# First token transform in 64 points on two row tiles, gate on four column tiles, column 0 turned by TensorE

## The chip, the core and the metric

The kernel runs on one core of a Trainium2 chip. The core has TensorE (PE in the profile, with its weight loads as PEld), VectorE (DVE), ScalarE (ACT), GpSimd (POOL) and SyncE (SP, which here only issues DMAs). The metric is the device time of one execution in microseconds, and of several runs the median.

## The reference, cut to what matters

The input x has 2048 tokens by 1024 channels. Two branches read it, and a gate for each token mixes them.

```
X = rfft2(x) * (w_r + 1j*w_i);  a = irfft2(X)                    # spectral branch
Bu = x @ B_bar.T;  h[t] = Lam_bar * h[t-1] + Bu[t]               # state branch
b = 2 * real(h @ C.T) + x * Dskip
g = sigmoid(sum(x * gate_w, -1));  out = g * a + (1 - g) * b
```

## The kernel before, in words

**Layout.** A token s is written as s = 16 p + j: partition p (128), row j (16). Each row j of x is loaded with 128 tokens on the partitions (`load_x`, L197, two rows at a time, eight loads), transposed by TensorE and copied by ACT into `xQ` (`turn_x`, L651).

**Spectral branch, front.** For each row j, `fold` (L657, DVE) and `fd` (L334) do the transform over channels: matmuls into `ps_fd` and a copy by ACT to X1. Then `s1` (L348) does the first transform over tokens: 128 points over p, with the twiddles in the constant `T3` (cosine, sine, minus sine; loaded by `load_T3` into the tile `raw`). Four matmuls of 512 columns, lines 351 to 354, give a real and an imaginary half. The result is copied to A1 (L356; by DVE for j < 10, by ACT after), of which there are four buffers, and stored to a scratch in DRAM (L358, `turn_scratch` in the profile). From there it is read back with the tokens turned, and `s2` (L457) does the second transform, of 16 points, as a matmul with the constant K2; then comes the product with the weights, and the way back through a second scratch (steps "is1" and "is2").

**Column 0.** The first channel frequency packs two real columns and has its own path: `keep_A1` (L362) collects it in Acol; POOL sends Acol to DRAM and reads it back turned as Bcol (L369, L372); the matmuls `zps` (L417 to L420) with the constant `K3` do the second transform for it, and a chain of small DVE operations and matmuls (`Zp`, `Zrev`, `Q`, `Qn`) leads to the column that `s2` puts into X2.

**State branch.** `unit(c, q)` (L255) works on 256 tokens and half of the states: 64 matmuls in two halves into `psu` (L303, the moving operand is 16 runs of 16 tokens out of `xQ`), each copied by ACT to h (L305), then about 13 us of DVE work in seven pieces (rotation, two scans of 2.3 us, rotation back). The pieces are queued in `work` with a cost written by hand, and `vector(us)` (L314) emits pieces until as many microseconds are paid. `c_half` (L562) multiplies h with C into `ps_y`; `early` (L577) stores ten tiles' results for later, and the rest is joined with the spectral result at the end.

**Gate.** `gate(r0, n)` (L695) is called after rows 9, 11, 13 and 15, with four rows each: eight matmuls a row, with 128x128 of `xQ` as weights and one moving column, then a copy to `zsb` (L701). After the last one POOL sends `zsb` to DRAM (L703) and reads it back as `zt`, by token tiles (L705). `gate_end` (L707) turns `zt` into the factors gB, omg and grat; the copies `ye` of the early tiles (L586) need omg.

**Order.** On PE, DVE and ACT the order is the program's own: the work is under `manual_schedule`, and the text from L860 on interleaves a row of the front, one half of a unit or tile (`halves`) and the vector pieces by hand. The strings in `plan` (L771) say which of turn (T), fold (f), fd (F) and s1 (S) a row does; `order` (L763) says after which row the B, C and small constants are loaded. The order of the DMAs on SP and POOL is chosen when the kernel is built, from simulated times, and need not be that of the text: SP issues loads of B (L208, transposing DMAs) ahead of stores that the text has earlier. After the front, `step()` drives the spectral generator: "w" (halves of the weights' column and five half steps of the state branch), "z", "q", "qn", "s2", and so on.

**Memory.** The front's tiles lie in pools that are closed after row 15 (`after_ia`, L515), and the pools of the next stage take their place. PSUM: two slots `psA` for the spectral branch, one `psF` for the units in the front, two `psX` for transposes and the gate.

Of the kernel before, what the change touches and what calls it, by code (L numbers as in the profile page):

```python
# [13 lines left out]
FP32 = mybir.dt.float32  # L14
# [22 lines left out]
def _host_consts():  # L37

    d = np.arange(K)[:, None] + 0.5
    G = np.zeros((2, K, 2, H))  # L40
    for cls in range(2):
        k = 2 * np.arange(H)[None, :] + cls
        ang = 2 * np.pi * d * k / D
        G[cls, :, 0] = np.cos(ang)
        G[cls, :, 1] = -np.sin(ang)
    G[0, :, 1, 0] = (-1.0) ** np.arange(K)

    n = np.arange(H)[None, :] + 0.5
    Gi = np.zeros((2, 2, 2, P, H))
    for cls in range(2):  # L50
        for kb in range(2):
            k = 2 * (P * kb + np.arange(P)[:, None]) + cls
            ang = 2 * np.pi * k * n / D
            Gi[cls, kb, 0] = 2.0 * np.cos(ang)
            Gi[cls, kb, 1] = -2.0 * np.sin(ang)
    Gi[0, 0, 0, 0] = 1.0
    Gi[0, 0, 1, 0] = (-1.0) ** np.arange(H)
    Gi /= float(D * S)
    s1 = np.arange(P)[:, None, None]
    s2 = np.arange(16)[None, :, None]  # L60
    m1 = np.arange(P)[None, None, :]
    angT = 2 * np.pi * (((16 * s1 + s2) * m1) % S) / S
    Tc, Ts = np.cos(angT), np.sin(angT)
    p = np.arange(P)
    q = p // 8
    a = p % 8
    angK = 2 * np.pi * ((q[:, None] * q[None, :]) % 16) / 16
    delta = (a[:, None] == a[None, :]).astype(np.float64)
    Kc, Ks = delta * np.cos(angK), delta * np.sin(angK)
    f = np.arange(P)  # L70
    fs, fr, fa = f[:, None] // 8, (f[:, None] // 4) % 2, f[:, None] % 4
    hr, hm, ha = f[None, :] // 64, (f[None, :] // 4) % 16, f[None, :] % 4
    angF = 2 * np.pi * ((fs * hm) % 16) / 16
    K2 = (fa == ha) * np.where(fr == hr, np.cos(angF), np.where(fr == 1, 1.0, -1.0) * np.sin(angF))
    pp = (np.arange(P) % 64)[:, None, None]
    bb = np.arange(32)[None, :, None]
    nn = np.arange(64)[None, None, :]
    angM = 2 * np.pi * (((32 * pp + bb) * nn) % S) / S
    top = (np.arange(P) < 64)[:, None, None]
    Mre = np.where(top, np.cos(angM), -np.sin(angM))  # L80
    Mim = np.where(top, np.sin(angM), np.cos(angM))
    gr, gb, ga = f // 64, (f // 2) % 32, f % 2
    angR = 2 * np.pi * ((gb[:, None] * gb[None, :]) % 32) / 32
    R2 = (ga[:, None] == ga[None, :]) * np.where(gr[:, None] == gr[None, :], np.cos(angR),
                                                  np.where(gr[:, None] == 0, 1.0, -1.0) * np.sin(angR))
    R2 = R2.reshape(P, 64, 2).transpose(0, 2, 1).reshape(P, P)
    Sel = np.zeros((P, 2, 2, P))
    for h in range(2):
        for ri in range(2):
            Sel[2 * np.arange(64) + h, h, ri, 64 * ri + np.arange(64)] = 1.0  # L90
    J = np.zeros((P, P))
    J[np.arange(P), 127 - np.arange(P)] = 1.0
    P0 = np.zeros((P, P))
    P0[(128 - np.arange(P)) % 128, np.arange(P)] = 1.0
    b16 = lambda z: np.ascontiguousarray(np.asarray(z, dtype=np.float32).astype(ml_dtypes.bfloat16))
    return dict(
        Ge=b16(G[0, 0:H].reshape(2, P, 2, P, 2).transpose(1, 4, 0, 2, 3)),
        Go=b16(G[1].reshape(4, P, 2, P, 2).transpose(1, 0, 4, 2, 3)),
        Gi=b16(Gi.reshape(8, P, H).transpose(1, 0, 2)),
        T3=b16(np.stack([Tc, Ts, -Ts], axis=2)),  # L100
        K3=b16(np.stack([Kc, Ks, -Ks], axis=1)),
        MT=b16(np.concatenate([-Mim, Mre, Mim], axis=2)),
        KRS=b16(np.concatenate([K2, R2, Sel.reshape(P, 4 * P)], axis=1)),
        JP=b16(np.stack([J, P0], axis=1)),
    )
# [3 lines left out]
def kernel(  # L109
# [25 lines left out]
    cT3 = nc.inline_tensor(hc["T3"], name="c_T3").ap()  # L135
# [7 lines left out]
    turn1_dram = dram.tile([16, 2, P, K], BF16, name="turn1_scratch")  # L143
    turn2_dram = dram.tile([32, P, K], BF16, name="turn2_scratch")
    col0_dram = dram.tile([P, 16, 2], BF16, name="col0_scratch")
    z_dram = dram.tile([P, 16], FP32, name="z_scratch")
# [43 lines left out]
    x_v = x.rearrange("(p j) d -> p j d", j=16)  # L190
# [4 lines left out]
    fft["T3"] = raw.rearrange("p (j t m) -> p j t m", t=3, m=P)  # L195

    def load_x(i):  # L197
        nc.sync.dma_start(out=xn[i], in_=x_v[:, 2 * i:2 * i + 2, :])

    def load_T3(a, b):  # L200
        nc.sync.dma_start(out=fft["T3"][:, a:b], in_=cT3[:, a:b])

# [50 lines left out]
    work = []  # L253

    def unit(c, q):  # L255
# [43 lines left out]
        for ri in range(2):  # L299
            psu = pools["u"].tile([P, 4, TC], FP32, name="psu", tag="psu")  # L300
            for j in range(4):
                for d8 in range(8):
                    nc.tensor.matmul(psu[:, j, :], lhsT=BT[4 * q + j][:, ri, d8, :],  # L303
                                     rhs=xQ[:, d8, :, 16 * c:16 * (c + 1)], start=(d8 == 0), stop=(d8 == 7))
            nc.scalar.copy(out=u[:, ri].rearrange("p b (q j) -> p b q j", j=16),  # L305
                           in_=psu.rearrange("p b (j q) -> p b q j", j=16))
# [23 lines left out]
    def gfnet():  # L330
        T3_sb = fft["T3"]
        Acol = fx.tile([P, 16, 2], BF16, name="Acol")
# [15 lines left out]
        def s1(j):  # L348
            X1 = X1s.pop(j)
            psa = psA.tile([P, 2, K], FP32, name="ps_s1", tag="ps")  # L350
            nc.tensor.matmul(psa[:, 0, :], lhsT=T3_sb[:, j, 0, :], rhs=X1[:, 0, :], start=True, stop=False)
            nc.tensor.matmul(psa[:, 0, :], lhsT=T3_sb[:, j, 1, :], rhs=X1[:, 1, :], start=False, stop=True)
            nc.tensor.matmul(psa[:, 1, :], lhsT=T3_sb[:, j, 0, :], rhs=X1[:, 1, :], start=True, stop=False)
            nc.tensor.matmul(psa[:, 1, :], lhsT=T3_sb[:, j, 2, :], rhs=X1[:, 0, :], start=False, stop=True)
# [3 lines left out]
            nc.sync.dma_start(out=turn1_dram[j].rearrange("r m k -> m r k"), in_=A1)  # L358
# [3 lines left out]
        def keep_A1(j):  # L362
            nc.vector.tensor_copy(out=Acol[:, j, :], in_=A1s[j][:, :, 0])
# [5 lines left out]
        nc.gpsimd.dma_start(out=col0_dram, in_=Acol)  # L369
        Bcol = fx.tile([P, 16, 2], BF16, name="Bcol")  # L370
        with nc.allow_non_contiguous_dma(reason="tiny corner turn"):
            nc.gpsimd.dma_start(out=Bcol, in_=col0_dram.rearrange("(a b) j c -> j a b c", a=8))  # L372
# [4 lines left out]
        Kc_sb, Ks_sb, Kns_sb = fft["K3"][:, 0], fft["K3"][:, 1], fft["K3"][:, 2]  # L377
        Wc = fft["Wc"]
        KRS_sb = fft["KRS"]
        t1_v = turn1_dram.rearrange("j r (a b) k -> (j r a) b k", a=4)  # L380
# [34 lines left out]
        yield "w"  # L415
        zps = psA.tile([P, 2, 16], FP32, name="zps", tag="ps")
        nc.tensor.matmul(zps[:, 0, :], lhsT=Kc_sb, rhs=Bcol[:, :, 0], start=True, stop=False)  # L417
        nc.tensor.matmul(zps[:, 0, :], lhsT=Ks_sb, rhs=Bcol[:, :, 1], start=False, stop=True)
        nc.tensor.matmul(zps[:, 1, :], lhsT=Kc_sb, rhs=Bcol[:, :, 1], start=True, stop=False)
        nc.tensor.matmul(zps[:, 1, :], lhsT=Kns_sb, rhs=Bcol[:, :, 0], start=False, stop=True)  # L420
# [94 lines left out]
    def after_ia():  # L515
# [7 lines left out]
        fft["wp"] = bctx.enter_context(tc.tile_pool(name="wp", bufs=1, side="right", reuse_waits="tile"))  # L523
        fft["Sel"] = fft["gt"].tile([P, 4, P], BF16, name="Sel_sb", tag="gc1", bufs=2)
# [152 lines left out]
    load_T3(0, 2)  # L677
    load_x(1)
    load_x(2)
    load_T3(2, 8)  # L680
    for i in range(3, 8):
        load_x(i)
    load_T3(8, 16)
# [8 lines left out]
    zsb = cpool.tile([P, 16], FP32, name="zsb")  # L692
    zt = cpool.tile([P, 16], FP32, name="zt")

    def gate(r0, n):  # L695
        zps = psX.tile([P, n], FP32, name="zps_g", tag="pt")
        for r in range(r0, r0 + n):
            for d8 in range(8):
                nc.tensor.matmul(zps[:, r - r0:r - r0 + 1], lhsT=xQ[:, d8, r, :], rhs=gwT[:, d8:d8 + 1],
                                 start=(d8 == 0), stop=(d8 == 7))  # L700
        nc.scalar.copy(out=zsb[:, r0:r0 + n], in_=zps)  # L701
        if r0 + n == 16:
            nc.gpsimd.dma_start(out=z_dram, in_=zsb)  # L703
            with nc.allow_non_contiguous_dma(reason="gate by token tiles"):
                nc.gpsimd.dma_start(out=zt, in_=z_dram.rearrange("(t a) j -> (a j) t", a=8))  # L705
# [14 lines left out]
    fft["K3"] = fx.tile([P, 3, P], BF16, name="K3_sb")  # L720
# [3 lines left out]
    def load_small():  # L724
        nc.sync.dma_start(out=fft["K3"], in_=cK3)
        nc.sync.dma_start(out=fft["JP"], in_=cJP)
        nc.sync.dma_start(out=fft["KRS"], in_=cKRS.rearrange("p (i m) -> p i m", m=P)[:, 0:2])
# [75 lines left out]
    gwT = vecT[:, 4]  # L803
# [56 lines left out]
    while at[0] < 16:  # L860
# [6 lines left out]
        if j in (9, 11, 13, 15):  # L867
            gate(2 * (j - 9), 4)
# [10 lines left out]
    for v, n in (("w", 5), ("z", 2), ("q", 2), ("qn", 1), ("s2", 0), ("uv", 1)):  # L879
# [91 lines left out]
```

## Time and profile before

| what | value |
|---|---|
| median of 7 runs | 348.69 us (347.09 to 350.62) |
| the profiled execution | 347.07 us, its span 345.3 us |
| PE busy | 329.0 us, 95% of the span |
| DVE busy | 298.0 us, 86% |
| ACT busy | 167.4 us, 48% |
| POOL busy | 34.4 us, 10% |
| mean granted clock of TensorE | 0.993 |
| DMA | 59.30 MB, 172 GB/s over the span |
| s1's matmuls, L351 to L354 | 64 of 128x512, 379 ns each as recorded, 0.215 us from start to start |
| gate's matmuls, L699 | 128 of one column, 163 ns each as recorded |
| psu's matmuls, L303 | 1024 of 256 columns, 117.7 us in all |

A matmul's record contains the way through the array, so records overlap; the cost of one in a stream is the distance of the starts. The chain of waits is read from the end backwards: each piece is what released the next. A DMA is on the queue of the engine that issued it; "DMA share" is the mean busy share of the core's 16 DMA engines, and may be over 1 where records overlap. "Released by" names what came last of the things that an instruction waited for.

### The profile page before, as it was taken

How to read it: one execution, taken by the hardware profiler on the slowest of the kernel's cores; microseconds unless marked ns; L12 is line 12 of the kernel's file. 1: busy time of each engine (PE TensorE's matmuls, PEld its weight loads, DVE VectorE, ACT ScalarE, POOL GpSimd, SP SyncE). 2: the span in 40 equal slices, each digit the busy share in tenths (PEclk: the TensorE clock that was granted, in tenths of full speed). 3: DMA queues.
4: the chain of work that ended last, by engine and by line, in shares of the span. 5: the costliest groups of instructions: out<-in, count | busy, mean ns of one | idle time of the engine just before them, and what ended most of it. 6: DMA issues, size and time to landing. Idle time of an engine off the chain costs nothing.

```text
span 345.3 us, 6604 instructions
## 1 busy us (share of the span) xinstructions
PE 329.0 (95%) x2593; PEld 226.8 (66%) x2593; DVE 298.0 (86%) x509; ACT 167.4 (48%) x215; POOL 34.4 (10%) x66
## 2 busy tenths in 40 slices
PE   7889599969999999999999999999999999999995
PEld 4666378858876675666647475596857885665652
DVE  2779687999997999999999999999646999999951
ACT  3798576575331225556646562365633333434410
POOL 1372011020021000000000000000000002112220
PEclk9999989999999999999999999999999999999999
DMA  7999999998793134869999953986601009866694
GB/s 289 392 219 177 222 211 201 188 243 213 232 195 49 63 91 100 248 186 248 294 205 308 238 163 107 245 186 166 178 2 61 2 0 163 133 103 130 116 153 151
DMA packets 83743, 59.30 MB, mean 172 GB/s; under 512 B 54368, under 2 KB 74496, under 8 KB 83584
## 3 DMA queue, kind: packets, MB, share of 16 engines
q1 hardware_dynamic: 80400, 56.20, 64.8%
q0 software_dynamic: 3232, 2.67, 8.1%
q8 instruction: 20, 0.33, 0.4%
q14 instruction: 11, 0.09, 0.1%
q10 hardware_dynamic: 80, 0.01, 0.0%
HBM read 31.06 MB, written 17.84 MB: 142 GB/s over the span
## 4 chain that ended last, share of the span: by engine, by line
PE 70%; DVE 16%; ACT 5%; DMA 5%; issue 3%; POOL 0%; ACTq 0%; DVEq 0%
PE ps_y L568 24%; PE psu L303 23%; PE ps_h L568 4%; PE ps_id L599 4%; DVE h L277 3%; PE ps_is L509 2%; PE ps_s L460 2%; PE ps_is L485 2%; PE ps_is L484 2%; ACT xQ L655 2%; DMA z_scratch<-zsb 2%; PE ps_y L572 2%; DVE A L356 1%; PE ps_fd L342 1%; DMA zt<-z_scratch 1%
## 5 line engine op out<-in xcount | busy, mean ns | idle before, releaser
L303 PE MATMUL psu<-xQ,BT 128*128 128x256 bf16 x1024 | 117.7, 275 | 3.9 <-ACT zsb L701 2.6
L303 PEld LDWEIGHTS <-BT 128*128 128x128 bf16 x1024 | 100.6, 99 | 20.4 <-issue 5.1
L568 PE MATMUL ps_y<-CT,h 128*128 128x512 bf16 x448 | 101.3, 379 | 0.0
L568 PEld LDWEIGHTS <-h 128*128 128x128 bf16 x512 | 49.6, 98 | 55.4
L277 DVE TENSOR_TENSOR_SCAN h<-rz,h 128x1024 bf16<-128x1024 f32 x32 | 72.4, 2281 | 0.3
L305 ACT CAST h<-psu 128x1024 bf16<-128x1024 f32 x32 | 32.3, 1010 | 57.8 <-PE psu L303 57.8
L614 POOL DMA_DIRECT2D BT<-y_scratch x10 | 12.1, 1206 | 211.9 <-ACT BT L602 178.1
L586 ACT ACTIVATE ye<-ps_y,omg 128x512 f32<-128x512 f32 x20 | 12.7, 684 | 33.1 <-PE ps_y L572 22.6
L264 DVE TENSOR_TENSOR su<-h,tab 128x2048 bf16<-128x2048 bf16 x16 | 19.6, 1223 | 8.0 <-ACT h L305 5.4
L462 ACT CAST X<-ps_s 128x1024 bf16<-128x1024 f32 x16 | 16.2, 1014 | 8.7 <-PE ps_s L460 8.7
L265 DVE TENSOR_TENSOR h<-h,tab 128x2048 bf16<-128x2048 bf16 x16 | 19.6, 1225 | 0.8
L290 DVE TENSOR_TENSOR h<-h,tab 128x2048 bf16<-128x2048 bf16 x16 | 19.6, 1225 | 0.5
L289 DVE TENSOR_TENSOR sg<-h,tab 128x2048 bf16<-128x2048 bf16 x16 | 19.5, 1218 | 0.0
L345 ACT CAST X<-ps_fd 128x1024 bf16<-128x1024 f32 x16 | 16.2, 1016 | 4.9 <-PE ps_fd L342 4.8
L511 ACT CAST ZT<-ps_is 128x1024 bf16<-128x1024 f32 x16 | 15.4, 1021 | 5.1 <-issue 3.0
L655 ACT COPY xQ<-pt 128x1024 bf16<-128x1024 bf16 x16 | 15.9, 1023 | 2.7 <-PE pt L654 2.7
L342 PE MATMUL ps_fd<-Go_sb,preT 128*128 128x256 bf16 x128 | 16.6, 273 | 0.0
L356 DVE CAST A<-ps_s 128x1024 bf16<-128x1024 f32 x10 | 12.2, 1218 | 4.8 <-DMA turn_scratch<-A 2.5
L487 ACT CAST C<-ps_is 128x1024 bf16<-128x1024 f32 x16 | 16.1, 1007 | 0.0
L599 PE MATMUL ps_id<-raw,ZT 128*128 128x256 bf16 x128 | 15.9, 273 | 0.0
L568 PE MATMUL ps_h<-CT,h 128*128 128x512 bf16 x64 | 14.5, 379 | 0.0
L599 PEld LDWEIGHTS <-ZT 128*128 128x128 bf16 x128 | 12.4, 98 | 2.2
(196 smaller groups left out, 414.4 us busy)
## 6 DMA issues: line engine op xcount, KB each, us to landing
y_scratch<-ye SPq DMA_DIRECT2D x20, 256.0 KB, 2.6
CT<-in_A_x_dram SPq DMA_DIRECT2D x8, 512.0 KB, 6.1
turn_scratch<-A SPq DMA_DIRECT2D x16, 256.0 KB, 4.4
Bb<-turn_scratch SPq DMA_DIRECT2D x16, 256.0 KB, 4.0
turn_scratch<-C SPq DMA_DIRECT2D x16, 256.0 KB, 2.7
raw<-turn_scratch SPq DMA_DIRECT2D x16, 256.0 KB, 4.4
Wb<-in_A_w_r_dram SPq DMA_DIRECT2D x32, 127.8 KB, 4.2
Wb<-in_A_w_i_dram SPq DMA_DIRECT2D x32, 127.8 KB, 3.8
```

Of the source, the lines that this page charges most:

```text
L264: nc.vector.tensor_mul(out=su, in0=u[:, ::-1], in1=bc(1))
L265: nc.vector.tensor_mul(out=u, in0=u, in1=bc(0))
L277: nc.vector.tensor_tensor_scan(out=seg, data0=rz[:, js].rearrange("p j t -> p (j t)"), data1=seg, initial=0.0, op0=ALU.mult, op1=ALU.add)
L289: nc.vector.tensor_mul(out=sg, in0=u[:, ::-1], in1=bc(3))
L290: nc.vector.tensor_mul(out=u, in0=u, in1=bc(2))
L303: nc.tensor.matmul(psu[:, j, :], lhsT=BT[4 * q + j][:, ri, d8, :], rhs=xQ[:, d8, :, 16 * c:16 * (c + 1)], start=(d8 == 0), stop=(d8 == 7))
L305: nc.scalar.copy(out=u[:, ri].rearrange("p b (q j) -> p b q j", j=16), in_=psu.rearrange("p b (j q) -> p b q j", j=16))
L342: nc.tensor.matmul(ps[:, q, H:K], lhsT=preTs[j][:, 4 + d4, :], rhs=fft["Go"][:, d4, q, :], start=(d4 == 0), stop=(d4 == 3))
L345: nc.scalar.copy(out=X1.rearrange("p r (i m) -> p r i m", m=4), in_=ps.rearrange("p q (c r i) -> p r i (q c)", c=2, r=2))
L568: nc.tensor.matmul(psy, lhsT=hs[c, jb // 4][:, ri, jb % 4, P * tq:P * (tq + 1)], rhs=CT[ri][:, jb, 512 * dh:512 * (dh + 1)], start=(i == 0 ...
L599: nc.tensor.matmul(pse[:, slot, :], lhsT=ZT_t[:, i, tb, :], rhs=fft["Gi"][:, i, :], start=(kb == 0), stop=(kb == 1))
L655: nc.scalar.copy(out=xQ[:, :, j, :], in_=pt)
```

## The change

A token is now s = 32 q + 16 g + j, and the partition of x is p = 64 g + q: the lower half of the partitions holds g = 0, the upper g = 1. The first transform has 64 points over q. Each half of the partitions is one row tile of the PE array (64 rows, 128 columns: real and imaginary part side by side), with a bank of PSUM of its own; two matmuls for each half take the place of the four over 128 rows. The constant T2 has two parts where T3 had three. The second transform has 32 points; K2 has other numbers and the same shape. x is loaded with two DMAs in place of each one. The unit's moving operand is 32 runs of 8 tokens.

The gate is one call after row 10 in place of four: gate_w is spread over 32 columns (gw32, a DVE copy), and four column tiles of 32 columns each take 512 tokens of `xQ` as moving operand, for eight blocks of channels: 32 matmuls. One copy by ACT and two DMAs of POOL follow at once.

Column 0: Acol is transposed by TensorE (`aps`), two DVE copies make Bcol (real, imaginary, minus real), and `zps` takes sixteen matmuls of 32 rows in place of four. The transpose and the copies are a step "a" of their own, one half step of the state branch ahead of "z"; "w" has four half steps in place of five. The constant K3 (64 KB) is loaded in `after_ia`, ahead of Sel, no longer after row 10.

```diff
-    turn1_dram = dram.tile([16, 2, P, K], BF16, name="turn1_scratch")
+    turn1_dram = dram.tile([32, P, K], BF16, name="turn1_scratch")
...
-    x_v = x.rearrange("(p j) d -> p j d", j=16)
+    x_v = x.rearrange("(p g j) d -> g p j d", g=2, j=16)
...
-    fft["T3"] = raw.rearrange("p (j t m) -> p j t m", t=3, m=P)
+    fft["T2"] = raw[:, 0:4 * D].rearrange("p (j t m) -> p j t m", t=2, m=P)
     def load_x(i):
-        nc.sync.dma_start(out=xn[i], in_=x_v[:, 2 * i:2 * i + 2, :])
+        for g in range(2):
+            nc.sync.dma_start(out=xn[i][64 * g:64 * (g + 1)], in_=x_v[g, :, 2 * i:2 * i + 2, :])
...
+    x_t = xQ.rearrange("p d j (g q) -> p d g j q", g=2)
...
-                                     rhs=xQ[:, d8, :, 16 * c:16 * (c + 1)], start=(d8 == 0), stop=(d8 == 7))
-            nc.scalar.copy(out=u[:, ri].rearrange("p b (q j) -> p b q j", j=16),
-                           in_=psu.rearrange("p b (j q) -> p b q j", j=16))
+                                     rhs=x_t[:, d8, :, :, 8 * c:8 * (c + 1)], start=(d8 == 0), stop=(d8 == 7))
+            nc.scalar.copy(out=u[:, ri].rearrange("p b (q j) -> p b q j", j=32),
+                           in_=psu.rearrange("p b (j q) -> p b q j", j=32))
...
-            nc.tensor.matmul(psa[:, 0, :], lhsT=T3_sb[:, j, 0, :], rhs=X1[:, 0, :], start=True, stop=False)
-            nc.tensor.matmul(psa[:, 0, :], lhsT=T3_sb[:, j, 1, :], rhs=X1[:, 1, :], start=False, stop=True)
-            nc.tensor.matmul(psa[:, 1, :], lhsT=T3_sb[:, j, 0, :], rhs=X1[:, 1, :], start=True, stop=False)
-            nc.tensor.matmul(psa[:, 1, :], lhsT=T3_sb[:, j, 2, :], rhs=X1[:, 0, :], start=False, stop=True)
+            for r in range(2):
+                for g in range(2):
+                    half = slice(64 * g, 64 * (g + 1))
+                    nc.tensor.matmul(psa[:, g, :], lhsT=T2_sb[half, j, r, :], rhs=X1[half, r, :],
+                                     start=(r == 0), stop=(r == 1), tile_position=(64 * g, 0))
...
-            nc.sync.dma_start(out=turn1_dram[j].rearrange("r m k -> m r k"), in_=A1)
+            nc.sync.dma_start(out=t1_w[j], in_=A1)
...
-        nc.gpsimd.dma_start(out=col0_dram, in_=Acol)
-        Bcol = fx.tile([P, 16, 2], BF16, name="Bcol")
-        with nc.allow_non_contiguous_dma(reason="tiny corner turn"):
-            nc.gpsimd.dma_start(out=Bcol, in_=col0_dram.rearrange("(a b) j c -> j a b c", a=8))
...
+        aps = psA.tile([32, P], BF16, name="aps", tag="ps")
+        nc.tensor.transpose(out=aps, in_=Acol.rearrange("p g j -> p (g j)"), identity=ident)
+        Bcol = fx.tile([32, 3, 4, 16], BF16, name="Bcol")
+        nc.vector.tensor_copy(out=Bcol[:, 0:2].rearrange("j c a b -> j (c a b)"), in_=aps)
+        nc.vector.tensor_scalar_mul(out=Bcol[:, 2], in0=Bcol[:, 0], scalar1=-1.0)
+        yield "a"
         zps = psA.tile([P, 2, 16], FP32, name="zps", tag="ps")
-        nc.tensor.matmul(zps[:, 0, :], lhsT=Kc_sb, rhs=Bcol[:, :, 0], start=True, stop=False)
...
+        for c, parts in enumerate((((Kc_sb, 0), (Ks_sb, 1)), ((Kc_sb, 1), (Ks_sb, 2)))):
+            for i in range(8):
+                lhs, r = parts[i // 4]
+                nc.tensor.matmul(zps[:, c, :], lhsT=lhs[:, i % 4, :], rhs=Bcol[:, r, i % 4, :], start=(i == 0), stop=(i == 7))
...
+        fft["K3"] = fft["gt"].tile([32, 2, 4, P], BF16, name="K3_sb", tag="gc1", bufs=2)
+        nc.sync.dma_start(out=fft["K3"], in_=cK3)
...
-    def gate(r0, n):
-        zps = psX.tile([P, n], FP32, name="zps_g", tag="pt")
-        for r in range(r0, r0 + n):
-            for d8 in range(8):
-                nc.tensor.matmul(zps[:, r - r0:r - r0 + 1], lhsT=xQ[:, d8, r, :], rhs=gwT[:, d8:d8 + 1],
-                                 start=(d8 == 0), stop=(d8 == 7))
-        nc.scalar.copy(out=zsb[:, r0:r0 + n], in_=zps)
...
+    def gate():
+        zps = psX.tile([P, K], FP32, name="zps_g", tag="pt")
+        for d8 in range(8):
+            for i in range(4):
+                nc.tensor.matmul(zps[32 * i:32 * (i + 1), :], lhsT=gw32[:, d8, :], rhs=xQ[:, d8, 4 * i:4 * (i + 1), :],
+                                 start=(d8 == 0), stop=(d8 == 7), tile_position=(0, 32 * i))
+        nc.scalar.copy(out=zsb.rearrange("p (q g j) -> p q g j", g=2, j=4), in_=zps.rearrange("p (j g q) -> p q g j", j=4, g=2))
+        with nc.allow_non_contiguous_dma(reason="gate by token tiles"):
+            nc.gpsimd.dma_start(out=z_dram.rearrange("(n i j) -> i n j", i=4, j=4),
+                                in_=zsb[0:P:32, :].rearrange("i (n j) -> i n j", j=4))
+            nc.gpsimd.dma_start(out=zt, in_=z_dram.rearrange("(t p) -> p t", p=P))
...
-        nc.sync.dma_start(out=fft["K3"], in_=cK3)
...
-        if j in (9, 11, 13, 15):
-            gate(2 * (j - 9), 4)
+        if j == 10:
+            gate()
...
-    for v, n in (("w", 5), ("z", 2), ("q", 2), ("qn", 1), ("s2", 0), ("uv", 1)):
+    for v, n in (("w", 4), ("a", 1), ("z", 2), ("q", 2), ("qn", 1), ("s2", 0), ("uv", 1)):
```

## The prediction

> **What bounds the kernel now.** I read the busy time by stage first, then the chain of waits, then the queue that the chain points at.
>
> ```profile
> 35.00:45.00 10.00, 5.92 (x38) 3.97 (x38) 6.60 (x17) 4.14 (x8) 0.61 (x1) 0.93 1.09 217
> ...
> 57.00:72.00 15.00, 12.84 (x132) 10.38 (x130) 14.54 (x23) 11.03 (x20) 2.80 (x5) 1.00 1.10 209
> 72.00:95.00 23.00, 22.32 (x253) 18.93 (x253) 22.58 (x38) 11.22 (x15) 0.20 (x4) 1.00 0.87 230
> 95.00:113.00 18.00, 17.65 (x137) 12.63 (x135) 15.87 (x37) 5.12 (x7) 3.46 (x4) 1.00 0.68 117
> 113.00:254.00 141.00, 141.00 (x1051) 93.14 (x1050) 132.28 (x175) 72.85 (x96) 0.00 (x0) 1.00 0.69 185
> ```
>
> After the stretch and its length the columns are PE, weight loads, DVE, ACT, POOL, the granted clock, the DMA share, GB/s. From 72 us on PE hardly stops: a saving there counts, but only there. From 57 to 72 DVE is full. In 35 to 45 neither is, while the DMA engines are: that stage is where the front (rows j = 0 to 15 of the transforms) is lost or won. The chain of waits there:
>
> ```profile
> 38.29 3.23 DMA turn_scratch<-A
> 41.61 1.24 DVE A L356
> ...
> 44.01 5.06 PE psu L303 x32
> ```
>
> DVE was ready for the eviction of s1(7) at 39.08 and got its buffer at 41.5. A1 has four buffers; that one is free when the store of A1(3) has landed. The store was issued at 38.29, though A1(3) was done at 27.4. The queue of SP shows why:
>
> ```profile
> 13.03 0.39 SPq L358 DMA_DIRECT2D turn_scratch<-A  x1
> 13.46 4.34 SPq L208 DMA_TRANSPOSE BT<-in_B_B_re_dram  x1
> 17.91 0.51 SPq L358 DMA_DIRECT2D turn_scratch<-A  x1
> 18.47 7.64 SPq L208 DMA_TRANSPOSE BT<-in_B_B_re_dram  x3
> ...
> 34.17 4.02 SPq L208 DMA_TRANSPOSE BT<-in_B_B_re_dram  x3
> 38.29 0.53 SPq L358 DMA_DIRECT2D turn_scratch<-A  x1
> ```
>
> From 13.46 SP never rests. An unhindered transpose takes 1.3 us to issue; the first took 4.34 and the next three 2.5 each, because the loads of x and T3 were still draining. So whatever lengthens those loads moves the store of A1(3), and with it s1(8), the first unit's matmuls (psu, which ran 5.06 us at a lowered clock instead of 3.50) and all behind them.
>
> **The change, part by part.**
>
> *x in halves.* Eight loads of 512 KB over 128 partitions become sixteen of 256 KB over 64. SP's extra issues cost 8 x 0.40 = 3.2 us, in its idle time from 9.79 to 13.03: nothing. The bytes are the same, the rate need not be. The DMA view has 128-partition loads alone (10 to 19 us) and, late, loads of exactly the new shape, 64 partitions by 4 KB (221 to 226 us):
>
> ```profile
> DMA packets 901, 3.46 MB, mean 384 GB/s; under 512 B 103, under 2 KB 123, under 8 KB 900
> ```
>
> ```profile
> DMA packets 382, 1.25 MB, mean 251 GB/s; under 512 B 76, under 2 KB 76, under 8 KB 382
> ...
> q1 hardware_dynamic: 382, 1.25, 95.6%
> ...
> raw<-turn_scratch SPq DMA_DIRECT2D x2, 256.0 KB, 5.0
> ```
>
> The engines are as busy and move a third less, though both halves' loads follow each other. At full share that is 251 / 0.956 = 263 GB/s. x is 8 x 512 KB = 4.19 MB: 10.9 us at 384, 15.9 at 263, so **+5.0** (bounds 0, if the halves run as the whole, and +5.8 by the plain 251). T2 is 1,024 KB where T3 was 1,536: 0.52 MB / 384 = **-1.4**. Net +3.6 on the store of A1(3).
>
> [...]
>
> The first x tile lands later as well: one more issue (0.4) and 0.52 MB at 263 for 384 (0.6), so 1.0. It is hidden by the 2.5 us that DVE waits at 39.08; without that wait it costs 1.0.
>
> *First transform on two row tiles.* Four matmuls of 512 columns start 0.215 us apart: 0.86 per row. As two pairs side by side: 0.43. No row shows such a pair, nor the switch to it. The nearest row for emptying the array is the 16-column matmul zps: it lasts 0.17 though its neighbours start 0.02 apart, so about 0.15 per switch, two per row: 0.73. If nothing overlaps: 1.16. Bounds per row -0.43 to +0.30; I take -0.25, between the two paired values. On the chain stand s1(8) and s1(9) only: **-0.5** (bounds -0.9 to +0.6).
>
> [...]
>
> *Gate.* 128 matmuls of one column in four places (0.81 us each, by the next matmul's start) become 32 of 512 columns after row 10's unit half. Without overlap 32 x 0.215 = 6.9; four abreast 1.7; I take 2.3 and 0.3 for two switches, nearer to the pairs as the streams are independent. The gates of rows 9 and 11 leave (1.6), so PE is about 1.0 later before its wait for ACT:
>
> ```profile
> 72.45 3.65 PE L303 MATMUL psu<-xQ,BT 128*128 128x256 bf16 x32 [2.61 <-ACT zsb L701]
> ```
>
> Those 2.61 us hide it; ACT is late there because its table pieces wait for DVE. Without overlap PE is 5.6 later and 3.0 show. ACT copies 128x512 once (0.68, as the ye rows), in the 3.67 us that it idles before 68.15, and loses four copies of 0.16. The added copy gw32 (about 0.25) lies in DVE's 0.67 us wait for dt. POOL issues the two z transfers some 35 us sooner; behind the second one's wait (5.6 us for the first to land) may stand the table casts (69.36 and 70.67), needed by DVE at 78.94: 7.5 us of cover. Wb memsets follow, far from need. What of this is between 72 and 95: row 13's gate leaves PE (0.8) and s1(13), s1(14) gain 0.5. Row 15's gate and s1 gain nothing, for PE then waits for ACT's copy h (93.03 to 94.04) anyway.
>
> *Column 0 and the gate's end.* Two tiny transfers leave, and the wait for zt (7.0 on ACT, 1.6 on DVE); on PE only 0.35 of it showed, at 112.72. In their place stand one transpose (with a switch 0.3), two DVE copies (0.18 each) and sixteen small matmuls for four (0.03 apart, with a switch +0.6). The new wait: zps needs Bcol from DVE, in order behind the vector pieces. DVE's old times without its 1.6 wait: multiplications done 109.25, gate arithmetic to 110.1, join to 111.6, Bcol 112.0. PE's old time for zps with the transpose: 112.3, less the 1.3 it gained alone: 111.0. So PE waits 1.0, with the next unit half and all of PE behind it. Sum: -1.3 - 0.35 + 1.0 + 0.3 + 0.6 = **+0.2** (bounds -1.3, no switches and no wait; +1.6, nothing gained before).
>
> *K3* is one 64 KB load before Sel at 93.79: 0.47 us of SP's queue; the three Bb loads behind it are needed at 131. *Second transform in 32*: same matmuls, other constants, nothing. *Unit matmuls* read runs of 8 for 16: 512 contiguous columns cost 3.45 / 16 / 512 = 0.421 ns each, runs of 16 cost 3.49 / 32 / 256 = 0.426, so nothing, at most another 1% (+1.1). ACT's copy h reads PSUM at another stride; 1.01 us for h and 1.02 for the scattered X1 say nothing. *Clock* of the first psu: a longer idle could halve it (+1.9), a shorter one restore it (-1.6); I take 0.
>
> **Sum.** +5.0 - 1.4 - 0.5 + 0.2 = **+3.3 us**. The profiled execution took 347.07 us, its span 345.3; with the sum 350.4. The median of the runs is 348.69, 1.62 above that execution, so the forecast on its scale is **352.0**.
>
> **Rivals.**
> - *The halves run as the whole.* For it: the late loads read what was just written to DRAM, x does not. Then -1.4 - 0.5 + 0.2 = -1.7: 347.0. Two in ten, half of it beyond 0.5%.
> - *The store's wait vanishes: faster.* SP's order is chosen at build time, and in program order only one transpose stands before the store of A1(3), not eleven. If the new order issues it before 35.9 (39.08 less the 3.2 it takes to land), 2.5 of waiting and 1.6 of low clock go, s1 gives 0.5, the late first x tile costs 1.0, the end +0.2: -3.4, 345.3. Against it: the transposes stay free to go ahead. 18 in 100.
> - *The tiles do not run side by side* (the change doesn't do what it says): +0.6 for -0.5 at s1 and 3.0 for the gate: +7.4, 356.1. 12 in 100.
>
> The likeliest, slow halves, has 50 in 100; a tenth of it ends within 0.5%. About 0.5% (1.7 us) is what a measurement can tell from no change. Faster 0.18 + 0.09 = 0.27, same 0.10 + 0.05 = 0.15, slower 0.58. The range, 345.0 to 356.5, leaves out about half of the second rival and the top.
>
> **What would show it.** x's loads at about 260 GB/s before 25 us; the store of A1(3) issued near 42 and DVE's wait for it above 5 us; s1's matmuls in pairs at equal starts, 0.73 per row; the gate 2 to 3 us once; a PE wait of about 1 us at zps; 113 to 254 unchanged in length. Wrong it is if SP's order puts the stores ahead, or the DMA rate holds at 384.

## The result and the profile after

The changed kernel took 351.42 us (median of 23 runs, 347.07 to 353.96); the kernel before, in the same sittings, 347.84 (58 runs, 345.11 to 350.65). The ratio is 1.0066, with a 95% interval of 1.0042 to 1.0091: **slower**, by about 2.3 us. The ratios here go by the fast runs alone and so leave out eight of these 23, which lie more than 1.5% above the fastest; by the medians of all runs the difference is 3.6 us. The profiled execution took 347.45 us with a span of 345.7, so it is one of the fastest of the changed kernel. What it shows as a small loss is larger in most runs; the experiments return to that.

The busy time by stage, with the same columns as before the change. The first stage before:

```profile
5.00:20.00 15.00, 13.23 (x132) 9.96 (x130) 10.59 (x36) 10.90 (x15) 4.11 (x18) 1.00 1.04 386
```

and all of them after:

```profile
5.00:20.00 15.00, 12.30 (x131) 8.95 (x133) 10.78 (x37) 10.52 (x14) 3.48 (x16) 1.00 1.03 265
...
35.00:45.00 10.00, 7.69 (x64) 5.69 (x64) 9.26 (x23) 5.92 (x11) 3.49 (x8) 1.00 1.26 226
...
57.00:72.00 15.00, 12.70 (x118) 8.75 (x116) 14.86 (x29) 10.69 (x18) 4.28 (x5) 0.92 1.10 176
72.00:95.00 23.00, 21.72 (x201) 17.64 (x200) 22.48 (x41) 8.81 (x9) 1.39 (x7) 0.98 1.01 190
95.00:113.00 18.00, 15.18 (x120) 10.07 (x118) 15.84 (x30) 5.02 (x7) 0.00 (x0) 1.00 0.91 256
113.00:254.00 141.00, 141.00 (x1059) 93.35 (x1056) 129.77 (x172) 72.77 (x96) 0.00 (x0) 1.00 0.68 182
```

Two early stages differ. From 5 to 20 us the DMA engines are as full as before (share 1.03 against 1.04) and move 265 GB/s in place of 386. From 35 to 45 PE works 7.69 us in place of 5.92 and DVE 9.26 in place of 6.60: the stage that held the front up is now busy. The loss is in 95 to 113, where PE has 15.18 in place of 17.65. From 113 to 254 nothing has changed.

The queue of SP tells why, in two places. (In the rows, the tiles of x appear as `CT`, T2 and later MT as `raw`, after the memory that they lie in.) Early:

```profile
7.80 9.66 SPq L199 DMA_DIRECT2D CT<-in_A_x_dram  x10
17.99 0.33 SPq L202 DMA_DIRECT2D raw<-c_T  x1
19.06 3.75 SPq L362 DMA_DIRECT2D turn_scratch<-A  x3
23.45 1.61 SPq L209 DMA_TRANSPOSE BT<-in_B_B_re_dram  x1
27.82 0.37 SPq L362 DMA_DIRECT2D turn_scratch<-A  x1
```

The loads of x occupy SP until 17.5. But the fourth store, A1(3), now has one transpose in front of it, not eleven, and is issued at 27.82 in place of 38.29 (the line from before is in the prediction). DVE never waits for it; its first work on the unit (`su`) begins at 54.27 in place of 57.26. Late, the queue holds MT (`raw<-c_MT`), a constant of 1.5 MB whose first reader comes at 136.5 us, and right behind it `xs`, the first transposed tile of x, which `ps_y` needs. Before and after:

```profile
89.13 0.34 SPq L375 DMA_DIRECT2D raw<-c_MT  x1
...
90.64 3.09 SPq L560 DMA_TRANSPOSE xs<-in_A_x_dram  x1
```

```profile
95.56 0.42 SPq L375 DMA_DIRECT2D raw<-c_MT  x1
...
96.53 3.52 SPq L568 DMA_TRANSPOSE xs<-in_A_x_dram  x1
```

In the chain of waits:

```profile
96.24 0.24 SPq L362
96.53 8.32 DMA xs<-in_A_x_dram
104.90 0.40 PE ps_y L580 x4
```

and in PE's own timeline:

```profile
104.90 0.40 PE L580 MATMUL ps_y<-dgD,xs 128*128 128x128 bf16 x4 [2.82 <-DMA xs<-in_A_x_dram]
105.13 3.62 PE L576 MATMUL ps_y<-CT,h 128*128 128x512 bf16 x16
...
108.90 0.23 PE L417 MATMUL aps<-ident,Acol 128*32 128x128 bf16 x1
109.06 3.67 PE L305 MATMUL psu<-xQ,BT 128*128 128x256 bf16 x32
112.66 0.56 PE L426 MATMUL zps<-Bcol,K_sb 32*128 32x16 bf16 x16
```

PE reaches the first ps_y at 98.47, 2.6 us sooner than before (101.07). It then stands 2.82 us for `xs`, which SP issued at 96.53 (before: 90.64, and PE went through without a wait). At 105.13 it is where it was before at 104.96. The lead of the front is gone, and the few tenths at zps and the end remain as a loss.

### The profile page after: what moved, and what is told of

Same layout as the page of the kernel before. It is cut to its first block, busy times and chain, and to the rows that moved or that the text cites. A ratio compares the mean times of both kernels' runs of the same rounds, so it can differ in the third digit from the quotient of the medians.

```text
span 345.7 us, 6456 instructions
## 1 busy us (share of the span) xinstructions
PE 324.2 (94%) x2510; PEld 219.3 (63%) x2510; DVE 298.9 (86%) x512; ACT 167.8 (49%) x212; POOL 33.9 (10%) x64
## 4 chain that ended last, share of the span: by engine, by line
PE 76%; DVE 9%; ACT 6%; DMA 4%; issue 3%; SPq 0%; ACTq 0%; DVEq 0%
PE psu L305 28%; PE ps_y L576 25%; PE ps_h L576 4%; PE ps_id L607 4%; DMA xs<-in_A_x_dram 2%; PE ps_is L515 2%; PE ps_is L490 2%; PE ps_is L491 2%; PE ps_s L466 2%; PE ps_fd L345 2%; PE ps_y L580 2%; ACT h L307 2%; ACT xQ L663 2%; DVE A L360 1%; DMA CT<-in_A_x_dram 1%
## 5 line engine op out<-in xcount | busy, mean ns | idle before, releaser
L341 PE MATMUL ps_fd<-Ge_sb,preT 128*128 128x256 bf16 x64 | 9.6, 272 | 4.5 <-ACT X L348 3.1
```

## The experiments

Two theories stood against each other. **A**: the half-width loads of x make SP late, and PE pays for it at xs. **B**: the new matmul forms, their switches or the clock cost the time. Each ratio is to the kernel before on the same chip in the same sitting, which took 348.43 us beside e1 to e4, 347.04 beside e5 to e8 and 348.12 beside e9 to e12.

| run | what | median us | ratio, 95% interval |
|---|---|---|---|
| e1 | after, unaltered | 352.00 | 1.0101, 1.0067 to 1.0135 |
| e2 | after, whole x loads | 350.02 | 1.0050, 1.0027 to 1.0072 |
| e3 | before, x loads in halves | 353.85 | 1.0115, 1.0077 to 1.0152 |
| e4 | after, upper halves issued by POOL | 359.71 | 1.0337, 1.0297 to 1.0376 |
| e5 | after, 16 loads of one row tile, 128 partitions | 348.73 | 1.0052, 1.0026 to 1.0078 |
| e6 | e2 with seven A1 buffers | 344.15 | 0.9931, 0.9906 to 0.9956 |
| e7 | after, MT meant later (still ahead of xs) | 348.36 | 1.0040, 1.0003 to 1.0076 |
| e8 | before with seven A1 buffers | 345.05 | 0.9962, 0.9932 to 0.9993 |
| e9 | after, MT issued by ACT | 345.40 | 0.9924, 0.9896 to 0.9952 |
| e10 | e6, MT issued by ACT | 344.49 | 0.9902, 0.9864 to 0.9939 |
| e11 | after with seven A1 buffers | 351.56 | 1.0102, 1.0054 to 1.0150 |
| e12 | e6, second stage's matmuls twice | 345.35 | 0.9920, 0.9893 to 0.9947 |

### The changed kernel again

> The changed kernel once more, unaltered. In its first profile the first unit's DVE work began 3.0 us earlier than before and the half steps after the front 2.6 us earlier, and PE then lost 2.8 us waiting for the load xs of the first early tile, which SP issued 5.9 us later than before. Theory A (the loads of x over 64 partitions run at about 260 GB/s for 384, and SP's queue is some 6 us late from then on until that load): x again at about 260 GB/s between 5 and 20 us, xs again issued at 96 to 97 us, PE waiting 2 to 4 us for it, and a time about 2.3 us above before. Theory B (the new matmul forms cost it: drains at the tile switches and a lowered clock where PE idles): the loss lies in s1, the gate and lowered clocks before 95 us, and the wait for xs is not there every time.

352.0 us. Its profiled execution, the slowest of its six runs (354.41 us, span 352.6), shows the loss at full size:

```profile
108.92 0.61 PE L580 MATMUL ps_y<-dgD,xs 128*128 128x128 bf16 x4 [5.74 <-DMA xs<-in_A_x_dram]
109.32 6.41 PE L576 MATMUL ps_y<-CT,h 128*128 128x512 bf16 x16
```

xs landed 10.2 us after its issue at 98.70. PE stood 5.74 us, and the sixteen matmuls behind the wait took 6.41 us in place of 3.62, at a granted clock of 0.86 over 95 to 113. So the wait costs about 8.5 us here and 2.8 in the first profile. That the spread of this kernel's runs, 347 to 354 us, is the spread of this wait is likely but not shown: a run without a profile doesn't show its wait, and the kernel before, with no such wait in its profile, spreads from 345 to 351.

### Whole loads in the changed kernel

```diff
-        for g in range(2):
-            nc.sync.dma_start(out=xn[i][64 * g:64 * (g + 1)], in_=x_v[g, :, 2 * i:2 * i + 2, :])
+        nc.sync.dma_start(out=xn[i], in_=x.rearrange("(p j) d -> p j d", j=16)[:, 2 * i:2 * i + 2, :])
...
-        nc.scalar.copy(out=xQ[:, :, j, :], in_=pt)
+        nc.scalar.copy(out=xQ[:, :, j, :].rearrange("p d (g q) -> p d g q", g=2),
+                       in_=pt.rearrange("p d (q g) -> p d g q", g=2))
```

> The changed kernel with x loaded in eight loads over 128 partitions: token 16 p + j on partition p as before, and ACT's copy out of the transposes puts p = 2 q + g into place 64 g + q, so all that follows is unaltered. Theory A: x at about 380 GB/s, T2 and the transposing loads start about 5 us earlier on SP, xs is issued at about 91 us, no PE wait for it; the time falls 2 to 4 us below the changed kernel, to 1 us above to 2 us below before, since the order of the stores on SP goes back towards that of before. Theory B: the matmul forms stay, so the time stays 2 us above before. A slower permuted copy would show as more than 1.02 us in ACT's copies.

350.02 us. x comes at 352 GB/s and PE doesn't wait for xs (it waits 1.67 us at the same place, for `dgD`, which DVE makes). The old wait is back, and longer:

```profile
40.80 3.57 DMA turn_scratch<-A
44.47 1.24 DVE A L359
```

SP's order is chosen at build time. With whole loads, twelve transposes stand ahead of the store of A1(3) (in the kernel before eleven, with halves one). `su` begins at 59.41. So the loads set two things, their own rate and the place of the stores, and these pull in opposite directions.

### Half loads in the kernel before

```diff
-        nc.sync.dma_start(out=xn[i], in_=x_v[:, 2 * i:2 * i + 2, :])
+        for g in range(2):
+            nc.sync.dma_start(out=xn[i][64 * g:64 * (g + 1)], in_=x_v[64 * g:64 * (g + 1), 2 * i:2 * i + 2, :])
```

> The kernel before with one part of the change alone: each load of x as two loads over 64 partitions, the same tokens in the same places. Theory A: x at about 260 GB/s; the stores of A1 come ahead of most transposing loads on SP, so that the wait of 2.5 us for the store of A1(3) goes and DVE starts the first unit 1 to 3 us earlier; xs is issued 5 to 7 us later and PE waits for it; together 0 to 3 us slower than before. Theory B: nothing of the new matmul forms is here, so no slower than before, or 1 to 3 us faster by the earlier stores.

353.85 us, ratio 1.0115: the half loads alone, with no new matmul form, bring at least the whole loss. In the profile the stores on SP stand as in the changed kernel, with one transpose ahead of A1(3), and PE waits 6.2 us for xs. (That execution took 355.82 us, near the top of this run's 349.27 to 356.38, so its times are read as a sign only.) Against B.

### The upper halves from another engine

```diff
-        for g in range(2):
-            nc.sync.dma_start(out=xn[i][64 * g:64 * (g + 1)], in_=x_v[g, :, 2 * i:2 * i + 2, :])
+        nc.sync.dma_start(out=xn[i][0:64], in_=x_v[0, :, 2 * i:2 * i + 2, :])
+        nc.gpsimd.dma_start(out=xn[i][64:128], in_=x_v[1, :, 2 * i:2 * i + 2, :])
```

> The changed kernel with the loads of x for the upper 64 partitions issued by POOL, those for the lower 64 by SP, so that the two halves are on the way at one time. Theory A with the half width as the cause of the rate: about 350 GB/s or more in 5 to 20 us, xs without a wait, 2 to 3 us faster than the changed kernel. If the rate is low because of the smaller loads, whatever partitions they go to: about 260 GB/s again and no gain. POOL's own work (rz, table casts) may come later; it has 8 us of idle time there.

359.71 us. The rate from 5 to 20 us stays at 268 GB/s with two engines issuing; the store of A1(3) now has sixteen transposes ahead of it. PE waits 5.0 us for tiles of x and 11.2 for A. Another issuing engine is no remedy; whether the width of the loads or their number slows them, the next run tells.

### As many loads, but over all partitions

```diff
+        for r in range(2):
+            nc.sync.dma_start(out=xn[i][:, r:r + 1, :], in_=x.rearrange("(p j) d -> p j d", j=16)[:, 2 * i + r:2 * i + r + 1, :])
```

(in place of the load of e2, with its copy)

> The kernel after, but x comes as 16 loads of one row tile each over all 128 partitions (256 KB, 2 KB to a partition), and the copy out of PSUM permutes the tokens, as in the whole load; as many loads as the changed kernel has, as large as its own, but not halved in partitions. A1, the half width is what slows x: 5 to 20 us run at 340 to 390 GB/s, the wait for xs in the front of the SSM is below 1 us, and the time is that of the kernel with whole loads, 349.5 to 350.5. A2, the number or the size of the loads is what slows x: 255 to 285 GB/s and 351 to 353. B, the new matmul forms: no change of the x loads matters, 351 to 352.

348.73 us, ratio 1.0052, as with whole loads. The stage from 5 to 20 us:

```profile
5.00:20.00 15.00, 13.08 (x132) 9.45 (x130) 10.96 (x38) 11.03 (x15) 3.98 (x18) 1.00 1.00 363
```

With sixteen loads of 256 KB this stage runs at 363 GB/s over 128 partitions, and at 265 over 64. It is the half width (A1). The store of A1(3) has twelve transposes ahead of it again, as in e2, and PE waits 6.0 us for A. So it is the width, and not the number of loads, that changes SP's order too.

### Both costs taken away

```diff
-            A1 = gta.tile([P, 2, K], BF16, name="A1", bufs=4)
+            A1 = gta.tile([P, 2, K], BF16, name="A1", bufs=7)
...
-    idle = gta.tile([P, K], BF16, name="idle", tag="A1", bufs=4)
+    idle = gta.tile([P, K], BF16, name="idle", tag="A1", bufs=7)
```

> The kernel after with whole x loads and seven buffers for A1 in place of four, so that no PSUM copy has to wait for a store behind the transposes. If the two costs are the half loads (paid at xs) and the place of the stores (paid by DVE), both are gone: PE's waits for A, 8.3 us before, below 2, DVE's first su by 54.5 us, no wait for xs over 1 us, and a time of 345.0 to 347.5, ratio 0.990 to 0.998. If the matmul forms or what follows the front cost the rest, it stays at 349 to 350.5 although the waits are gone.

344.15 us, ratio 0.9931, faster than both kernels. The store of A1(3) still goes out late, at 40.94, but no copy waits for it: PE's waits for A fall from 8.3 us in e2 to 1.5. `su` begins here:

```profile
53.62 1.23 DVE L265 TENSOR_TENSOR su<-h,tab 128x2048 bf16<-128x2048 bf16 x1 [2.18 <-ACT h L306]
```

xs is issued at 90.32 and PE doesn't wait for it. Part of the gain is the buffers', which e8 gives to the kernel before; beside it, the change without its half loads costs nothing.

### MT later, a miss

```diff
-        nc.sync.dma_start(out=MT_sb, in_=cMT)
...
         loads = [load(0), load(1), load(2)]
         yield "w"
+        nc.sync.dma_start(out=MT_sb, in_=cMT)
```

> The kernel after with its own half loads; only the load of MT (1.5 MB, which SP issues ahead of xs) is issued after the first Bb and Wb loads. A: xs lands 3 to 6 us sooner, PE's wait of 2.8 to 5.7 us for it falls below 1, with it the lowered clock after it, and the time falls to 347 to 349.5 (control 352.0). B, or a loss that is not paid at xs: 351 to 352.5 whatever the wait does. A rival within A: MT lands late for its first reader at 136.5 us, or Bb is late; then PE waits there and 351 or more remains.

348.36 us, ratio 1.0040. The edit moved a line of the program and not the load: SP's build-time order still has MT (issued at 93.22) ahead of xs (94.82). The run is a second control, and its interval overlaps that of the result. It tells nothing of MT. It shows the spread: the profiled execution had a wait of 1.1 us for xs and a span of 344.3, while the runs reached 353.68.

### Seven buffers in the kernel before

> The kernel before with seven buffers for A1 in place of four and nothing else: what the wait of A for the fourth store is worth by itself. If it sets the end of the front: DVE's first su 2 to 3 us sooner (57.26 before), and 345.0 to 346.5, ratio 0.990 to 0.995. If PE then waits for xs or another load in its place, as the changed kernel does at 104.9 us: 347.5 to 348.7, the same as before.

345.05 us, ratio 0.9962. The edit is that of e6. `su` begins at 53.31, 4.0 us sooner, and PE reaches the first ps_y at 98.86, 2.2 sooner; about 1.3 us of it is left in the ratio, a smaller gain than the 0.990 to 0.995 expected. Part of the lead is lost behind zps, in a wait that was 0.35 us with four buffers:

```profile
111.74 3.65 PE L303 MATMUL psu<-xQ,BT 128*128 128x256 bf16 x32 [1.79 <-ACT ye L586]
```

`ye` needs the gate, whose z took 5.9 us from issue to landing in the scratch and 4.3 on the way back.

### xs freed, half loads kept

```diff
         loads = [load(0), load(1), load(2)]
         yield "w"
+        nc.scalar.dma_start(out=MT_sb, in_=cMT)
```

(and the load on SP taken out; ACT's order is that of the program)

> The kernel after with its own half loads; the 1.5 MB of MT are issued by ACT behind the first ye copies, some 15 us later than SP issued them, so that xs no longer follows them in the queue (the edit of e7_late_MT left SP's order as it was, with MT ahead of xs, so that it was a second run of the kernel after). A: xs, issued at 96.53 and landed 8.3 us later with MT ahead of it, lands 2 to 5 us sooner, PE's wait for it falls below 0.8 us in the profile, and the ratio to before, 1.004 to 1.010 with MT ahead, falls to 0.996 to 1.002; the spread of the runs, 346 to 354 us, narrows too. B, or a loss that is paid elsewhere: 1.004 to 1.010 although the wait is shorter. A rival within A: the loads of Wb and the transposes alone keep xs late; then the wait stays over 2 us.

345.40 us (344.77 to 347.04), ratio 0.9924, beside 351.56 for e11 on the same chip. MT is issued at 108.17. In SP's queue, and then on PE:

```profile
97.76 1.60 SPq L568 DMA_TRANSPOSE xs<-in_A_x_dram  x1
```

```profile
99.32 3.62 PE L576 MATMUL ps_y<-CT,h 128*128 128x512 bf16 x16
102.78 0.70 PE L580 MATMUL ps_y<-dgD,xs 128*128 128x128 bf16 x4
```

xs is issued no sooner than in the changed kernel (97.76 for 96.53). What changed is the landing. That of the first xs isn't recorded here, but PE reaches it at 102.78 without a stop, so it took 5.0 us at most; the later ones that are recorded took 3.1 to 4.2. Behind MT's 1.5 MB the first took 8.3 to 10.2 in the profiles of the result, e1, e7 and e11. One transfer, moved, turns the change from +0.7% to -0.8% with half loads, new forms and all. With e3, A is shown, and so is the place where it is paid. How much of SP's lateness is the loads' rate and how much the changed order was not separated.

### MT by ACT where xs was not late

> The kernel of e6_whole_buf7 with MT issued by ACT as well. There PE didn't wait for xs, so under A nothing is left to win: ratio 0.990 to 0.996, as e6. If MT's 1.5 MB cost something other than xs (Bb, the second and third xs): 0.985 to 0.990.

344.49 us, ratio 0.9902; the interval overlaps that of e6, so no gain is shown where there was no wait. By the medians it is 0.9 us below e9 on the same chip. That may be what the half loads still cost once xs is free of MT; the two differ in the buffers too.

### Seven buffers where the stores were not late

> The kernel after with its half loads and seven buffers for A1. Its stores already stand ahead of the transposes, so the buffers have nothing to take away: 1.003 to 1.010, as the kernel after. If a store still held DVE in the kernel after, or the copies run further ahead: 0.993 to 1.000. The difference between this and e6_whole_buf7 is then the whole price of the half loads with the stores' wait out of both: 2.5 to 5 us under A.

351.56 us, ratio 1.0102: nothing gained, and by the ratios 5.9 us above e6, more than the 2.5 to 5 expected. The profile shows the wait at its longest, and the slower matmuls behind it:

```profile
106.93 0.61 PE L580 MATMUL ps_y<-dgD,xs 128*128 128x128 bf16 x4 [6.48 <-DMA xs<-in_A_x_dram]
107.33 4.82 PE L576 MATMUL ps_y<-CT,h 128*128 128x512 bf16 x16
```

### What the second stage's matmuls are worth

```diff
-            for r in range(2):
+            for r in (0, 1, 0, 1):
```

> The kernel of e6_whole_buf7 with the four 64-row matmuls of the second stage issued twice in each row (the second pass starts anew and writes the same values), 16 rows of 0.54 us = 8.6 us more on PE in the front. If the front goes at PE's pace: 350 to 353. If it goes at DVE's, which is busy 37.3 of the 38 us from 57 to 95: at most 1.5 us more, 344 to 346, and then the 5 us of PE that the change takes out of the second stage are worth as little.

The second stage here is s1, the first transform over tokens. 345.35 us, ratio 0.9920; e6 had 0.9931, and e10, on the same chip, 344.49. A row of the changed kernel and a row here:

```profile
46.80 0.61 PE L357 MATMUL ps_s<-X,raw 64*128 64x512 bf16 x4
```

```profile
47.44 1.04 PE L356 MATMUL ps_s<-X,raw 64*128 64x512 bf16 x8
```

Four more matmuls cost 0.43 us, over 16 rows 6.9 us of PE (the expectation said 8.6), and the kernel ends between nothing and 0.9 us later. That is the net of several things. SP's order differs a little, and PE waits 0.88 us for xs, which it didn't in e6. On the other side, PE waits less ahead of the unit half at 69.92 (1.28 us for 2.29), and that half takes 3.65 us for the 5.32 of e6. So sixteen rows of matmuls cost little here, but what they would cost without these shifts isn't shown. Up to 57 us the front waits on loads, ACT and DVE by turns; from 57 to 95 DVE is busy 37.3 of 38 us.

## Why the prediction was right, and where it was not

The time came out as forecast, 351.42 for 352.0, slower for its reason (the half loads), but not by its path. The loss forecast was 3.3 us on a kernel before of 348.69; measured, the kernel before is at 347.84, and the loss 2.3 us by the ratio and 3.6 by the medians.

- **Rate of x: right.** 263 GB/s forecast, 265 measured over the stage (253 to 271 in other runs with halves) and 243 from 10 to 17 us, where SP issues nothing but x (395 before). The late loads of the same shape were the right row to read. T2's smaller size (-1.4) shows nowhere by itself. In e5, with as many loads over all 128 partitions, the stage ran at 363.
- **The step that failed: "whatever lengthens those loads moves the store of A1(3)".** The loads did end later, and the first store was issued at 19.06 for 13.03. But the store of A1(3) went out 10.5 us sooner, for the half loads also changed SP's build-time order, as the second rival had said; its point (issued before 35.9) was passed at 27.82. e3 shows that the loads alone do this, e5 that it is their width. What the sum took as +3.6 there was a gain of 3.0 at `su`.
- **What that rival missed.** It gave -3.4, and e9, where xs is free, is 2.6 us faster than before by its ratio. It did not follow the queue to its end: SP issued MT and xs some 6 us later than before, and xs, which before had been in time, took MT's 1.5 MB with it into PE's path: 2.8 us of waiting in the first profile, 1.1, 5.7 and 6.5 in e7, e1 and e11, with slower matmuls behind the longer two. This wait took back the front's lead of 2.6 us and brought the loss of 2 to 4 us besides. That the total agrees with a sum made for another place is luck: the half loads are the cause that was forecast, the wait is not.
- **First transform on two row tiles: size right, worth less.** A row occupies PE for 0.54 us (start to next start) in place of 0.86. The eight `ps_fd` matmuls ahead of it take 0.97 to the row's start (45.83 to 46.80) in place of 0.87 (49.34 to 50.21 before), so the row gains 0.22 for the 0.25 taken. The second pass of e12 costs 0.43 for two pairs, two abreast at 0.215 each, so about 0.11 of the 0.54 is left for leaving the form, and 0.10 ahead of the row for entering it: 0.21 for both, where the prediction reckoned 0.30. That 0.30 was the author's estimate from zps; whether the array is emptied at such a change no run shows. PE has about 3.5 us less work in sixteen rows (16 x 0.22). What that is worth at the end isn't shown; e12, where 6.9 us more cost 0.9 at most, with the shifts told there, makes it likely to be little.
- **Gate: right.** 32 matmuls from 57.81 to 59.65, 1.84 us for the 2.3 and 0.3 of switches forecast. PE still waits 2.30 us for ACT at the unit half behind it (69.42), so the gate is hidden. z landed late on POOL (zt waited 7.4), as foreseen, and nobody waited for the table casts.
- **Column 0: right in size by luck, wrong in its terms.** From the second half of ps_y to the unit half behind zps PE takes 8.02 us (105.13 to 113.15) for 7.76 before (104.96 to 112.72): +0.26. The forecast for this stretch was +1.55 (-0.35 + 1.0 + 0.3 + 0.6); its sum of +0.2 came of the -1.3 that PE was to gain earlier, and that went into the wait for xs. The 1.0 of waiting for Bcol did not come, not even in e6 and e9, where PE doesn't stand for xs. It was reckoned from DVE's old times, and DVE was ahead of them by then: the `su` at 106.76 before begins at 103.85.
- **Clock of the first psu (taken as 0, bounds +1.9 and -1.6): it came back.** It ran 3.67 us at 41.28, at a granted clock of 1.00, for 5.26 before at 43.81 (0.69), where PE had stood 2.22 us for A just ahead. The second rival had counted this 1.6. A later unit half went the other way: 5.32 us at 69.42 (0.68), 3.65 before at 72.45 (1.00). Behind the same wait of 2.3 us it took 5.3 in nine profiles and 3.65 in e2, e5 and e11; why is open.
- **The chances** enter the first rival, two in ten, as 0.09 and 0.10; nothing rests on the difference.

What is the change worth by itself, without the half loads? e6 against e8, seven buffers and whole loads in both, has 0.9931 (0.9906 to 0.9956) and 0.9962 (0.9932 to 0.9993), which overlap. But both ran on one chip in one sitting and can be compared directly: ten runs of 343.63 to 344.95 us against twelve of 343.98 to 348.16, medians 0.9 us apart, and of the twelve only one is below the median of the ten. So this build of the change is a little faster. In the profiles PE starts the unit half behind zps at 110.08 in e6 and at 111.74 in e8, where it has waited 1.79 us for `ye`; that points to the early gate. It isn't shown for any one part of the change.

## What to carry to other kernels

When a load early in a queue gets longer, follow that queue to its last entry before the lead-in ends, not only to the next wait: the price is paid at the first transfer that had no slack, here xs, 80 us later and behind 1.5 MB that nobody needed for another 30 us. Where a scheduler orders a queue at build time, a change in the shape of transfers can reorder the rest (here their width did, and their number did not), and moving a line may move nothing; look at the built order before and after. Saved matmuls can be worth little: in e12 6.9 us more of them on PE ended in 0.9 us at most, with DVE busy 37.3 of 38 us from 57 to 95. Doubling them gives a first idea, but look in the profile whether waits and clock have moved too.

## What was not expected of the hardware

- A wait of PE can cost more than its length. After 5.74 us the sixteen ps_y matmuls took 6.41 us, at a granted clock of 0.86 over 95 to 113; after 6.48 us 4.82 (0.81); after 2.82 us 3.62, as without one (1.00).
- A transposing load of 256 KB landed 3.0 to 4.2 us after its issue where recorded in e9 and e10, with MT on another queue (the first xs isn't among them), and the first xs 8.3 to 10.8 us behind the 1.5 MB load on the same queue (the result, e1, e2, e5, e6, e7, e11 and e12). In e6 it was 9.9, without harm, as xs had been issued at 90.32.
- Two engines that issue to the two partition halves (e4) hardly raise the rate: 268 GB/s for 265 from 5 to 20 us.
